# Regrouping the heads of an mLSTM kernel so that S runs in four quarter tiles, with one transfer for q and k, two state copies, and an earlier zeroing of the output

## The chip, the cores and the metric

The kernel runs on 1 core of one Trainium2 chip. The metric is the device time of one execution in microseconds (us). Before the change the median of 3 runs is 236.06 us (235.61 to 236.2).

## What is computed

The reference is a recurrent attention over 4 batches, 8 heads, 768 steps and a head width of 40, followed by a mixture of 8 experts:

```python
for t in range(S):
    m_new = np.maximum(f_gate[:, :, t] + m, i_gate[:, :, t])
    f_stab = np.exp(f_gate[:, :, t] + m - m_new)
    i_stab = np.exp(i_gate[:, :, t] - m_new)
    C = f_stab * C + i_stab * outer(v, k)          # per head, 40 x 40
    n = f_stab * n + i_stab * k
    y[:, :, t] = sigmoid(o_gate) * (C @ q) / max(abs(n @ q), 1)
...
logits = x @ w_gate                                # x: 3072 tokens of 320
expert_idx = np.argmax(logits, axis=1)
for e in range(8):
    # of the tokens of expert e the 80 with the largest gate weight are kept
    h = np.maximum(x[tok_idx] @ w1[e], 0.0)
    out[tok_idx] = gate_w * (h @ w2[e])            # all other rows stay 0
```

## The kernel before

**The work.** The recurrence is done in 12 chunks of 64 steps. The 32 heads stand as 16 groups g of two members y; the members of a group lie in the two 64-row halves of the 128 partitions. A half-step i is one chunk and 8 of the groups (16 heads), so there are 24 half-steps. For each of them there are these steps, named as in the order strings:

- `s` (`s_s`, L384): S = k·q of the 64 x 64 steps of each head, 16 matmuls. Their weights are 128 rows, in which the rows of the other member are zeros, so that the 128 rows of the moving side may hold both members' q. They run in tiles of 128 rows and 64 columns; y picks the column half. The result stands in one of two rotating banks.
- `w` (`s_arg`, L364): the decay weights, a matmul `ar` of two small tables `lh` and `rc`, and an exp on ACT. The tables come by way of DRAM: DVE makes `lb`, `store_d2` (L324) writes it out, `load_lh` (L329 to L332) and `load_rc` (L346) read it back in other shapes.
- `p` (`s_p`, L398): P = S times w, on DVE. `pv` (`s_pv`, L406): P times v, 8 matmuls of 82 columns. `int` (`s_int`, L418): q times the state, 8 matmuls of 82 columns. `st` (`s_st`, L427): the state's increment.
- `post` (`s_post`, L435 to L450): the two parts added, divided and gated, on DVE and POOL. `state` (`s_state`, L477 to L487): the new state `cs`, and four copies of 40 x 164 that put it as `cb` in the form that `int` takes; ACT makes them, or DVE and POOL in the half-steps of `OFF`.
- `tp`, `xt`, `z`, `lg`: transposes, their copies, and the gate logits; `xd` (L534) stores y to DRAM for the gather later.

**The inputs.** `load_qk` (L127 to L130) loads a chunk's q and k with two DMAs of 40 partitions x 8 KB, one for each member; three buffers rotate. Since the weights of `s` are read with all their 128 rows, the rows that no DMA writes must be zero: the function `zeros` (L158 to L170) writes those gaps once for each of the three buffers, the pieces dealt out to DVE (L164), ACT (L168) and POOL (L170). `load_kv` (L134 to L136) loads k and v in natural form, into two rotating buffers.

**The order.** It is written by hand. The string `PRE` orders the first half-steps and all that is made once, the string `BODY` is run for i = 2 to 21, and `TAIL` orders the last two half-steps. In a `BODY` of half-step i, `s` makes S of i+2 and `p` makes P of i+1. Every engine takes its instructions in that order; all DMAs but a few are issued by SP, which takes its rows in order too and holds back a row, and all rows behind it, until the row's semaphores are there. After `TAIL` comes the choice of the tokens (DVE and PE), four weight loads (L155), `zero_out` (L769 to L771: four DMAs of 960 KB that fill the output with zeros), the gather of the chosen rows by 8 indirect DMAs of POOL (L972), and the two expert layers (L1002 to L1064), whose results are scattered into the zeroed output.

The functions that the change touches, and what calls them:

Of the kernel before, what the change touches and what calls it, by code (L numbers as in the profile page):

```python
# [72 lines left out]
def tile_mlstm_moe(ctx, tc, cap, qk_d, kn_d, vn_d, og_d, if_d, cst_d, cs2_d, zr_d, wz_d, w1_d, w2_d, out_d, dbg=None):  # L73
# [53 lines left out]
    def load_qk(c):  # L127
        j = c % NQ
        SP.dma_start(qk_b[j][0:40, 0:2], qk_d[c, 0])
        SP.dma_start(qk_b[j][64:104, 1:3], qk_d[c, 1])  # L130
# [26 lines left out]

    def zeros(eng, t, *spans):  # L158
        for r0, r1, a, b in spans:
            d = t[r0:r1, a:b].rearrange("r a g t -> r (a g t)") if len(t.shape) == 4 else t[r0:r1].rearrange("r g t -> r (g t)")  # L160
            if eng is V:
                z = zb.bitcast(F32)[r0:r1]
                d = d.rearrange("r (k n) -> r k n", n=z.shape[1])
                V.tensor_copy(d, z.unsqueeze(1).broadcast_to(list(d.shape)))  # L164
            elif eng is A:
                z = zb[r0:r1]
                d = d.rearrange("r (k n) -> r k n", n=z.shape[1])
                A.copy(d, z.unsqueeze(1).broadcast_to(list(d.shape)))  # L168
            else:
                eng.memset(d, 0.0)  # L170
# [213 lines left out]
    def s_s(i):  # L384
        c, hb = divmod(i, 2)
        qk = qk_b[c % NQ]
        sp = ps.tile([128, 4, 2, T], F32, tag="s", name=f"s{i}")
        for q in range(4):
            for x in range(2):
                g = 8 * hb + 2 * q + x  # L390
                for y in range(2):
                    TE.matmul(sp[64 * y:64 * y + 64, q, x], lhsT=qk[:, 2 * y, g], rhs=qk[:, 1, g], start=True, stop=True)  # L392
# [1 line left out]
        st["p", i] = (pp, sp.rearrange("r q x t -> r (q x) t"))

    def s_p(i):
        pp, sp = st["p", i]
        V.tensor_tensor(pp, sp, st.pop(("w", i)), ALU.mult)  # L398

    def s_pv(i):  # L400
        c, hb = divmod(i, 2)
        pp, _ = st.pop(("p", i))
        hp = (ps if i == NHS - 1 else ps1).tile([128, 4, 2, V1], F32, tag="s" if i == NHS - 1 else "h", name=f"h{i}")
        for p in range(8):
            r0 = 64 * (p % 2)
            TE.matmul(hp[r0:r0 + 64, p // 2], lhsT=pp[:, p], rhs=vb[c % NV][:, :, 8 * hb + p], start=True, stop=True)  # L406
# [64 lines left out]
    def s_state(i):  # L471
        c, hb = divmod(i, 2)
        if c == NC - 1:
            return
        gs = gs_(i)
        if c:
            V.tensor_tensor(cs[:, 4 * hb:4 * hb + 4], cpv, st.pop(("cg", i)), ALU.add)  # L477
        else:
            V.tensor_copy(cs[:, 4 * hb:4 * hb + 4], cpv)
        cbv = cb.rearrange("r y (q x) v -> r y q x v", x=2)  # L480
        for x in range(2):
            for y in range(2):
                dst, src = cbv[64 * y:64 * y + 40, y, 4 * hb:4 * hb + 4, x], cs[64 * x:64 * x + 40, 4 * hb:4 * hb + 4, y]
                if i in OFF:
                    (V if x == y else P).tensor_copy(dst, src)
                else:
                    A.copy(dst, src)  # L487
# [281 lines left out]
    def zero_out(k):  # L769
        SP.dma_start(out_d.rearrange("(p r) d -> p (r d)", p=128)[:, 1920 * k:1920 * (k + 1)].rearrange("p (r n) -> p r n", n=480),  # L770
                     zt.unsqueeze(1).broadcast_to([128, 4, 480]))  # L771
# [338 lines left out]

def constants():
# [93 lines left out]
```

## Time and profile before

| | |
|---|---|
| median of 3 runs | 236.06 us |
| the profiled execution | 237.19 us |
| its span, first to last instruction | 235.4 us |
| mean granted TensorE clock | 0.901 |
| busy: PE, DVE, ACT, POOL | 197.7, 132.4, 92.3, 102.4 us |
| DMA | 52.13 MB, mean 221 GB/s |

The profile comes from one execution. PE is TensorE's matmuls, PEld its weight loads, DVE VectorE, ACT ScalarE, POOL GpSimd, and SPq the queue of DMA issues of SyncE. A row of the timeline gives the start and the duration in us, the engine, the line of the kernel, the operation, what it writes and reads, the tile or shape, and how many instructions the row gathers; in brackets stands idle time ahead of it, with what ended it. A row of SPq shows when a DMA was issued, not when it landed. By its stages the execution is: about 0 to 30 us the first half-steps and all that is made once, 30 to 78 and 78 to 131 the half-steps in `BODY`, 131 to 142 the tail, 142 to 162 the choice of the tokens, then the gather and the experts.

### The profile page before, as it was taken

The page shows a single profiled execution, that of the slowest core. Times are in us where ns is not written, and L with a number is a line of the kernel's source. Part 1 is how long each engine was busy: PE and PEld are TensorE (multiplying, and loading weights), DVE is VectorE, ACT ScalarE, POOL GpSimd, SP SyncE. Part 2 cuts the span into 40 slices and gives each one's busy share as a digit, 9 for nine tenths or more (in the row PEclk, how much of TensorE's full clock was granted, in tenths as well). Part 3 has the DMA queues.
Part 4 walks back from the last instruction along what each step waited for, and adds up shares of the span by engine and source line. Part 5 has one row for each costly group of instructions (what it writes and reads, how often), then busy time and mean ns, then how long its engine had stood idle before and what let it go on. Part 6 is the DMA issues. An engine that isn't in the chain of part 4 may idle for free. (4 is left out here: it accounts for less than half of the span.)

```text
span 235.4 us, 7898 instructions
## 1 busy us (share of the span) xinstructions
PE 197.7 (84%) x3315; PEld 147.2 (63%) x3315; DVE 132.4 (56%) x394; ACT 92.3 (39%) x215; POOL 102.4 (44%) x169
## 2 busy tenths in 40 slices
PE   6695766988695999989899887789549999999991
PEld 2375556766584788778687764434339964699540
DVE  8999855898494396998689988773000001000000
ACT  4657614679463886536455533000012210022000
POOL 8955743868576077567627514003720001110111
PEclk9659977999999799999999999555958999999998
DMA  4976389978997977869999349999379999900010
GB/s 116 230 224 135 96 187 226 256 184 226 232 248 192 225 218 176 190 165 217 320 248 284 98 95 380 421 361 383 98 227 426 424 421 414 405 35 3 0 58 14
DMA packets 21968, 52.13 MB, mean 221 GB/s; under 512 B 4972, under 2 KB 13996, under 8 KB 19180
## 3 DMA queue, kind: packets, MB, share of 16 engines
q1 hardware_dynamic: 21116, 49.72, 69.6%
q0 software_dynamic: 672, 1.64, 2.2%
q8 instruction: 26, 0.43, 0.8%
q10 hardware_dynamic: 144, 0.26, 0.4%
q14 instruction: 10, 0.08, 0.1%
HBM read 42.65 MB, written 9.12 MB: 220 GB/s over the span
## 5 line engine op out<-in xcount | busy, mean ns | idle before, releaser
L392 PEld LDWEIGHTS s<-qk 128*64 128x64 f32 x768 | 27.8, 154 | 12.5 <-issue 4.7
L392 PE MATMUL s<-qk 128*64 128x64 f32 x768 | 31.2, 242 | 4.7 <-DMA qk<-in_qk 3.7
L1064 POOL DMA_INDIRECT out<-ob,iqi x6 | 5.8, 975 | 54.3 <-DVE ob L1061 40.6
L1025 PE MATMUL hp<-cx,w 128*64 128x80 f32 x512 | 25.1, 242 | 4.2 <-DVE cx L1004 3.7
L450 POOL TENSOR_TENSOR xn<-u,rd 128x320 f32<-128x320 f32 x23 | 17.1, 747 | 25.3 <-DVE u L449 22.2
L487 ACT COPY cb<-cs 40x164 f32<-40x164 f32 x76 | 25.1, 330 | 6.7 <-DVE cs L477 4.5
L1025 PEld LDWEIGHTS hp<-cx,w 128*64 128x64 f32 x512 | 23.6, 144 | 4.7 <-DVE cx L1004 3.9
L1057 PE MATMUL op<-w,ht 128*64 128x320 f32 (+1 forms) x256 | 26.4, 433 | 0.0
L381 POOL TENSOR_TENSOR kw<-kv,w 128x320 f32<-128x320 f32 x22 | 17.1, 778 | 14.5 <-DMA kv<-in_kn 8.2
L1061 DVE TENSOR_SCALAR ob<-op,iq 128x320 f32<-128x320 f32 (+1 forms) x6 | 3.1, 523 | 33.1 <-PE op L1057 33.1
L406 PE MATMUL h<-kv,p 128*64 128x82 f32 x384 | 19.1, 242 | 1.9 <-DVE p L398 1.4
L1057 PEld LDWEIGHTS op<-w,ht 128*64 128x64 f32 (+1 forms) x256 | 12.6, 117 | 12.7 <-issue 4.3
L1044 ACT ACTIVATE ht<-hp 128x320 f32<-128x320 f32 x16 | 7.0, 437 | 33.1 <-PE hp L1025 33.1
L418 PE MATMUL hib<-cb,qk 128*64 128x82 f32 x336 | 16.5, 240 | 2.8 <-issue 2.8
L366 ACT ACTIVATE w<-ar 128x512 f32<-128x512 f32 x22 | 13.1, 596 | 13.5 <-PE ar L364 13.3
L517 ACT COPY xt<-tp 128x384 f32<-128x384 f32 x20 | 9.5, 476 | 22.1 <-PE tp L502 22.0
L406 PEld LDWEIGHTS h<-kv,p 128*64 128x64 f32 x384 | 16.6, 143 | 2.3 <-issue 2.3
L435 DVE TENSOR_TENSOR hs<-hib,gn 128x328 f32<-128x328 f32 x21 | 10.4, 496 | 13.1 <-PE hib L418 12.9
L398 DVE TENSOR_TENSOR p<-s,w 128x512 f32<-128x512 f32 x24 | 16.4, 682 | 2.0 <-ACT w L366 1.1
L427 PE MATMUL cps<-kv,kw 128*40 128x82 f32 x352 | 17.2, 239 | 0.0
L972 POOL DMA_INDIRECT xg<-xd,idx x8 | 7.9, 982 | 19.3 <-DVE gi L980 17.2
L418 PEld LDWEIGHTS hib<-cb,qk 128*64 128x64 f32 x336 | 14.0, 140 | 3.3 <-issue 3.0
(213 smaller groups left out, 370.6 us busy)
## 6 DMA issues: line engine op xcount, KB each, us to landing
w<-in_w SPq DMA_DIRECT2D x14, 1280.0 KB
qk<-in_qk SPq DMA_DIRECT2D x24, 320.0 KB
kv<-in_vn SPq DMA_DIRECT2D x24, 164.0 KB
kv<-in_kn SPq DMA_DIRECT2D x12, 320.0 KB
xd<-xn SPq DMA_DIRECT2D x24, 160.0 KB
out<-zt SPq DMA_DIRECT2D x4, 960.0 KB
xn<-in_og SPq DMA_DIRECT2D x9, 320.0 KB
w<-in_w SPq DMA_DIRECT2D x4, 640.0 KB
```

The lines of the kernel that those rows point to most:

```text
L366: A.activation(w, ar, AF.Exp)
L381: P.tensor_tensor(kw, kn_b[c % NV][:, gs_(i)], st["w", i][:, :, T - 1:T].broadcast_to([128, 8, D]), ALU.mult)
L392: TE.matmul(sp[64 * y:64 * y + 64, q, x], lhsT=qk[:, 2 * y, g], rhs=qk[:, 1, g], start=True, stop=True)
L398: V.tensor_tensor(pp, sp, st.pop(("w", i)), ALU.mult)
L406: TE.matmul(hp[r0:r0 + 64, p // 2], lhsT=pp[:, p], rhs=vb[c % NV][:, :, 8 * hb + p], start=True, stop=True)
L418: TE.matmul(hi[r0:r0 + 64, p // 2], lhsT=qk_b[c % NQ][:, 1, g], rhs=cb[:, :, g], start=True, stop=True)
L427: TE.matmul(cpv[r0:r0 + 40, p // 2], lhsT=kw[:, p], rhs=vb[c % NV][:, :, 8 * hb + p], start=True, stop=True)
L435: V.tensor_tensor(hs, st.pop(("hi", i)), gn[:, c, gs].rearrange("r (q a) -> r q a", a=2).unsqueeze(3).broadcast_to([128, 4, 2, V1]), ALU.mult)
L450: P.tensor_tensor(xn[:, i], u, rd.broadcast_to([128, 8, D]), ALU.mult)
L487: A.copy(dst, src)
L1025: TE.matmul(out, lhsT=w[:, k, c0:c0 + 64], rhs=rhs, start=start, stop=stop)
L1057: TE.matmul(o[gw * j:gw * j + m, 0:DM], lhsT=hts[p][:, f, a, t0:t0 + m], rhs=w[:, a, f], start=(f == 0), stop=(f == 7), tile_position=(0, ...
```

## The change

**q and k.** On the host q and k are padded to 64 rows for each member and stacked, so a chunk is one array of 128 rows x 8 KB. It is loaded by one DMA (1 MB instead of 2 x 320 KB; chunk 0 by two, each with half of the groups). The function `zeros`, its constants and its nine entries in `PRE` are gone.

**S.** A matmul of S now takes the 40 rows of one member alone, and is put on a quarter of the array: the row half is y, the column half is h. In a row of the program y changes first, then h, so that four neighbours lie on four quarters. The heads are regrouped for this on the host and in the constant tables. S no longer has rotating banks: one tile `spb` of two banks holds both half-steps of a chunk, and y picks the bank.

**What follows from the grouping.** `s_pv` and `s_st` write their 82 columns as two runs of 41; in `s_pv` the column half now goes 0, 0, 1, 1 over its eight matmuls instead of 0, 1, 0, 1. `s_state` needs two copies of 40 x 328 instead of four of 40 x 164. The last half-step's PV goes to `spb`.

**The zeroing.** The four DMAs of `zero_out` move from behind the four weight loads to a new step `zero` of `BODY`, behind `xd`, at i = 20.

```diff
     def load_qk(c):
-        j = c % NQ
-        SP.dma_start(qk_b[j][0:40, 0:2], qk_d[c, 0])
-        SP.dma_start(qk_b[j][64:104, 1:3], qk_d[c, 1])
+        if c:
+            SP.dma_start(qk_b[c % NQ], qk_d[c])
+            return
+        for h in range(2):
+            SP.dma_start(qk_b[0][:, :, 8 * h:8 * h + 8], qk_d[0, :, :, 8 * h:8 * h + 8])
...
     def s_s(i):
...
-        sp = ps.tile([128, 4, 2, T], F32, tag="s", name=f"s{i}")
-        for q in range(4):
+        for b in range(2):
             for x in range(2):
-                g = 8 * hb + 2 * q + x
-                for y in range(2):
-                    TE.matmul(sp[64 * y:64 * y + 64, q, x], lhsT=qk[:, 2 * y, g], rhs=qk[:, 1, g], start=True, stop=True)
+                for h in range(2):
+                    for y in range(2):
+                        r = slice(64 * y, 64 * y + D)
+                        g = 8 * hb + 4 * b + 2 * h + x
+                        TE.matmul(spb[64 * h:64 * h + 64, y, hb, 2 * b + x], lhsT=qk[r, 0, g], rhs=qk[r, 1, g], start=True, stop=True)
...
     def s_pv(i):
...
         for p in range(8):
-            r0 = 64 * (p % 2)
-            TE.matmul(hp[r0:r0 + 64, p // 2], lhsT=pp[:, p], rhs=vb[c % NV][:, :, 8 * hb + p], start=True, stop=True)
+            b, x, y = p // 4, p // 2 % 2, p % 2
+            TE.matmul(hp[64 * x:64 * x + 64, 2 * b:2 * b + 2, y], lhsT=pp[:, p], rhs=vb[c % NV][:, :, 8 * hb + p], start=True, stop=True)
...
     def s_st(i):
...
-            r0 = 64 * (p % 2)
-            TE.matmul(cpv[r0:r0 + 40, p // 2], lhsT=kw[:, p], rhs=vb[c % NV][:, :, 8 * hb + p], start=True, stop=True)
+            b, x, y = p // 4, p // 2 % 2, p % 2
+            TE.matmul(cpx[64 * y:64 * y + 40, b, :, x], lhsT=kw[:, p], rhs=vb[c % NV][:, :, 8 * hb + p], start=True, stop=True)
...
     def s_state(i):
...
-        cbv = cb.rearrange("r y (q x) v -> r y q x v", x=2)
-        for x in range(2):
-            for y in range(2):
-                dst, src = cbv[64 * y:64 * y + 40, y, 4 * hb:4 * hb + 4, x], cs[64 * x:64 * x + 40, 4 * hb:4 * hb + 4, y]
-                if i in OFF:
-                    (V if x == y else P).tensor_copy(dst, src)
-                else:
-                    A.copy(dst, src)
+        for y in range(2):
+            r = slice(64 * y, 64 * y + 40)
+            dst, src = cb[r, y, 8 * hb:8 * hb + 8], cs[r, 4 * hb:4 * hb + 4].rearrange("r q x v -> r (q x) v")
+            if i in OFF:
+                (V if y else P).tensor_copy(dst, src)
+            else:
+                A.copy(dst, src)
...
+    def b_zero(i):
+        if i == ZO:
+            for k in range(4):
+                zero_out(k)
...
-    for k in range(4):
-        zero_out(k)
```

How the instructions stand now is shown at three places. A name is that of a buffer with a number; `[waits ...]` names the engines or DMA queues whose semaphores the row waits for.

The first is SP's queue at the start of the program, before: `gt` is the gates, `d` the DRAM copy of `lb`.

```order
L92 DMA gt<-in_gif 32x1536
L129 DMA qk_81<-in_qk 40x2048 [waits DVE_49]
L130 DMA qk_81<-in_qk 40x2048 [waits Pool_49]
L134 DMA kv_84<-in_kn 128x640
L324 DMA d_133<-lb 32x6x128 [waits DMAHW1_49,DVE_49]
L129 DMA qk_83<-in_qk 40x2048 [waits DMAHW2_49,Pool_49]
L130 DMA qk_83<-in_qk 40x2048 [waits DMAHW3_49,Pool_49]
L129 DMA qk_81<-in_qk 40x2048 [waits DMAHW4_49,PE_49]
L346 DMA rc_93<-d_133 3x16x128 [waits DMAHW6_49,DMAHW1_49,DVE_49]
```

The same queue now (the rows for chunk 1 lie between the fourth and the fifth in both):

```order
L92 DMA gt<-in_gif 32x1536
L134 DMA qk_81<-in_qk 128x2x512 x2
L138 DMA kv_84<-in_kn 128x640
L312 DMA d_134<-lb 32x6x128 [waits DVE_49]
L131 DMA qk_83<-in_qk 128x2048 [waits DMAHW1_49]
L131 DMA qk_81<-in_qk 128x2048 [waits DMAHW2_49,PE_49]
L334 DMA rc_94<-d_134 3x16x128 [waits DMAHW3_49,DMAHW0_49,DVE_49]
```

The transfers of q and k wait for no zeroing by DVE, POOL or ACT any more, and the rows for `rc` and `lh` behind them don't either.

The second is DVE in a half-step of `BODY`, from one state update (`cs`) to the next, before:

```order
L477 TENSOR_TENSOR cs<-cps,cg_1150 104x328 [waits Pool_49]
L398 TENSOR_TENSOR p_1113<-s_1096,w_1084 128x512 [waits Activation_49]
L435 TENSOR_TENSOR hs_1262<-hib,gn 128x328 [waits PE_49]
L437 TENSOR_TENSOR hs_1262<-h_1234,hs_1262 128x328 [waits DVE_49,PE_49]
L443 TENSOR_SCALAR rd_1265<-hs_1262 128x8 [waits DVE_49]
L445 TENSOR_TENSOR rd_1265<-hs_1262,rd_1265 128x8 [waits DVE_49]
L447 RECIPROCAL rd_1265<-rd_1265 128x8 [waits DVE_49]
```

The same stretch now:

```order
L470 TENSOR_TENSOR cs<-cps,cg_1102 104x328 [waits Pool_49]
L388 TENSOR_TENSOR p_1066<-spb,w_1040 128x512 [waits PE_49,Activation_49]
L428 TENSOR_TENSOR hs_1211<-hib,gn 128x328 [waits PE_49]
L430 TENSOR_TENSOR hs_1211<-h_1183,hs_1211 128x328 [waits DVE_49,PE_49]
L436 TENSOR_SCALAR rd_1214<-hs_1211 128x8 [waits DVE_49]
L438 TENSOR_TENSOR rd_1214<-hs_1211,rd_1214 128x8 [waits DVE_49]
L440 RECIPROCAL rd_1214<-rd_1214 128x8 [waits DVE_49]
```

No row moved, but `p` of half-step i+1 now waits for PE as well: the last matmul of S of i+2, which PE has written to the same two banks just ahead.

The third is SP's queue at the end of `BODY`, before (`zt` is the tile of zeros, `w` the experts' weights):

```order
L155 DMA w_0_1713<-in_w 128x1280
L134 DMA kv_85<-in_kn 128x640
L136 DMA kv_85<-in_vn 64x656 x2
L534 DMA xd<-xn 64x4x160 x6
L155 DMA w_1_2496<-in_w 128x2560 x2
L155 DMA w_0_2499<-in_w 128x2560 x2
L770 DMA out<-zt 128x4x480 x4
L981 DMA gid<-gi 96x16
```

The same stretch now:

```order
L159 DMA w_0_1644<-in_w 128x1280
L138 DMA kv_85<-in_kn 128x640
L140 DMA kv_85<-in_vn 64x656 x2
L526 DMA xd<-xn 64x4x160 x2
L756 DMA out<-zt 128x4x480 x4
L526 DMA xd<-xn 64x4x160 x4
L159 DMA w_1_2409<-in_w 128x2560 x2
L159 DMA w_0_2412<-in_w 128x2560 x2
L969 DMA gid<-gi 96x16
```

The zeros stand ahead of the last four stores of y and of four of the weight loads.

More of the change, by code (lines that the diff above doesn't have):

```diff
@@ L40 @@
 WH = [2, 0, 1, 0]
-BODY = "tab pr0 cmp s int pv tp st load xt xd cg p w post arg0 pr1 cnt pg z state d2 arg1 sig lh og lg"
+BODY = "tab pr0 cmp s int pv tp st load xt xd zero cg p w post arg0 pr1 cnt pg z state d2 arg1 sig lh og lg"
 PG = {11: (8, 10), 3: (4, 6), 9: (6, 8), 12: (10, 12)}
@@ L59 @@
 BW0 = [2, 2, 2, 2, 4]
+ZO = 20
 GATE = {7: (0, 2), 13: (2, 4), 15: (4, 6), 19: (6, 8), 21: (8, 9)}
@@ L100, in tile_mlstm_moe @@
     NV, NQ = 2, 3
-    qk_b = [cp.tile([128, 3, G16, T], F32, name=f"qk{i}") for i in range(NQ)]
+    qk_b = [cp.tile([128, 2, G16, T], F32, name=f"qk{i}") for i in range(NQ)]
     kv_b = [cp.tile([128, 2, VN + KN], F32, name=f"kv{i}") for i in range(NV)]
@@ L107, in tile_mlstm_moe @@
     cs = cp.tile([104, 8, 2, V1], F32, name="cs")
+    spb = ps1.tile([128, 2, 2, 4, T], F32, tag="s", name="spb")
     cps = ps1.tile([128, 512], F32, tag="cps", name="cps")
@@ L156, in load_w @@
             yield
[L158 to L168, printed above, removed]
-            else:
-                eng.memset(d, 0.0)
-    GAPS = ((32, 64, 0, 2), (64, 128, 0, 1), (96, 128, 1, 3), (0, 64, 2, 3))
     zb = gp.tile([128, 512], BF16, name="zb")
@@ L386, in s_s @@
         qk = qk_b[c % NQ]
[L387 to L388 removed]
+        for b in range(2):
             for x in range(2):
[L390 to L392 removed]
+                for h in range(2):
[3 more added lines that the diff above has]
+                        TE.matmul(spb[64 * h:64 * h + 64, y, hb, 2 * b + x], lhsT=qk[r, 0, g], rhs=qk[r, 1, g], start=True, stop=True)
         pp = wk.tile([128, 8, T], F32, tag="p", name=f"p{i}")
[L394 removed]
+        st["p", i] = (pp, spb[:, :, hb].rearrange("r y f t -> r f y t"))
     def s_p(i):
         pp, sp = st["p", i]
[L398 removed]
+        two = lambda a: a.rearrange("r (f y) t -> r f y t", y=2)
+        V.tensor_tensor(two(pp), sp, two(st.pop(("w", i))), ALU.mult)
     def s_pv(i):
@@ L402, in s_pv @@
         pp, _ = st.pop(("p", i))
-        hp = (ps if i == NHS - 1 else ps1).tile([128, 4, 2, V1], F32, tag="s" if i == NHS - 1 else "h", name=f"h{i}")
+        if i == NHS - 1:
+            hp = spb.rearrange("r y h f t -> r (y h f t)")[:, 0:8 * V1].rearrange("r (q y v) -> r q y v", y=2, v=V1)
+        else:
+            hp = ps1.tile([128, 4, 2, V1], F32, tag="h", name=f"h{i}")
         for p in range(8):
-            r0 = 64 * (p % 2)
-            TE.matmul(hp[r0:r0 + 64, p // 2], lhsT=pp[:, p], rhs=vb[c % NV][:, :, 8 * hb + p], start=True, stop=True)
+            b, x, y = p // 4, p // 2 % 2, p % 2
+            TE.matmul(hp[64 * x:64 * x + 64, 2 * b:2 * b + 2, y], lhsT=pp[:, p], rhs=vb[c % NV][:, :, 8 * hb + p], start=True, stop=True)
         st["h", i] = hp
@@ L798, in tile_mlstm_moe @@
                 z=b_z, state=s_state, pr1=b_prep(1), cmp=b_cmp, cnt=b_cnt, lg=b_lg, arg1=b_arg1, sig=s_sig, xd=b_xd, pg=b_pg,
-                load=b_load, lh=b_lh, og=b_og, d2=b_d2, tab=b_tab, w=b_w)
+                load=b_load, lh=b_lh, og=b_og, zero=b_zero, d2=b_d2, tab=b_tab, w=b_w)
     for i in range(2, NHS - 2):
@@ L1108, in constants2, with heads @@
     return c
+def heads(a):
+    return a.transpose(0, 2, 3, 1, *range(4, a.ndim)).reshape(32, *a.shape[4:])
 def constants():
@@ L1143, in constants @@
     put("dy", 0, dy.reshape(32, 2))
-    put("sel", 0, sel.reshape(32, 48))
-    put("ind", 0, ind.reshape(32, 104))
+    put("sel", 0, heads(sel.reshape(B, 2, 2, 2, 48)))
+    put("ind", 0, heads(ind.reshape(B, 2, 2, 2, 104)))
     return c
```

23 lines of the change are left out of this document (9 added, 14 removed).

## The prediction

> **What bounds the kernel now.** I read the busy time by stages first, since the shares over the whole span mix stages with different limits. The columns are PE, PEld, DVE, ACT and POOL busy, then PE's granted clock, the share of the DMA engines' time and GB/s.
>
> ```profile
> core 0: us, PE busy (x) PEld busy (x) DVE busy (x) ACT busy (x) POOL busy (x), PEclk, DMA share, GB/s
> 10.00:20.00 10.00, 8.81 (x102) 6.26 (x101) 9.75 (x22) 6.95 (x8) 7.21 (x7) 0.60 0.88 228
> 20.00:30.00 10.00, 6.72 (x147) 5.67 (x147) 8.71 (x31) 6.21 (x17) 6.11 (x9) 1.00 0.40 101
> 30.00:40.00 10.00, 6.41 (x95) 5.59 (x97) 5.26 (x11) 2.35 (x6) 2.63 (x5) 0.75 0.85 183
> 60.00:70.00 10.00, 8.20 (x182) 6.75 (x184) 7.04 (x25) 5.16 (x14) 6.21 (x18) 1.00 0.97 249
> 80.00:90.00 10.00, 10.00 (x223) 8.37 (x220) 8.03 (x22) 8.49 (x14) 5.94 (x12) 1.00 0.87 217
> 100.00:110.00 10.00, 9.10 (x208) 7.63 (x210) 9.06 (x34) 4.48 (x11) 6.39 (x13) 1.00 0.76 186
> 130.00:140.00 10.00, 8.64 (x155) 6.88 (x152) 9.14 (x38) 4.33 (x13) 3.24 (x5) 1.00 0.25 65
> 150.00:160.00 10.00, 7.88 (x61) 3.86 (x60) 7.16 (x18) 0.00 (x0) 0.00 (x0) 0.50 1.01 381
> ```
>
> Three limits follow one another. From 10 to 20 us DVE has no gap (9.75 of 10). From 30 to about 78 no engine is full and the DMA engines nearly are. From 80 on PE has no gap (10.00 of 10), with DVE at 8 to 9 behind it. In the timeline of the first stage the reader is to see the zero writes between the steps of the gate scan, and whom they hold up:
>
> ```profile
> 1.16 3.89 DVE L164 COPY qk<-zb 32x2048 f32<-32x2048 f32 x2
> 5.78 0.28 DVE L290 TENSOR_TENSOR_SCAN m<-gt 32x64 f32<-32x64 f32 x1
> 13.96 0.69 DVE L164 COPY qk<-zb 64x1024 f32<-64x1024 f32 x1
> 16.74 1.88 DVE L164 COPY qk<-zb 64x1024 f32<-64x1024 f32 x1
> 22.93 0.27 DVE L318 TENSOR_TENSOR lb<-rb,lb 32x128 bf16<-32x128 f32 x1
> 4.58 1.35 ACT L660 COPY xg<-cst 32x1024 f32<-32x1024 f32 x2 [1.92 <-DMA cst<-in_cst]
> 25.52 1.80 POOL L170 MEMSET qk<- 32x2048 f32 x1
> 23.23 0.33 SPq L324 DMA_DIRECT2D d<-lb  x1
> 23.66 0.32 SPq L129 DMA_DIRECT2D qk<-in_qk  x1
> 27.34 0.29 SPq L130 DMA_DIRECT2D qk<-in_qk  x1
> 28.49 1.46 SPq L346 DMA_DIRECT2D rc<-d  x2
> 31.69 1.97 PE L392 MATMUL s<-qk 128*64 128x64 f32 x32 [3.67 <-DMA qk<-in_qk]
> 37.71 0.10 PEld L364 LDWEIGHTS <-lh 118*128 118x128 bf16 x1 [2.06 <-DMA lh<-d]
> 75.07 0.10 PEld L364 LDWEIGHTS <-lh 118*128 118x128 bf16 x1 [2.90 <-DMA lh<-d]
> ```
>
> The store of `lb` is issued at 23.23, when DVE has made the last of it (22.93 + 0.27). The second q/k transfer of chunk 2 sits at SP until POOL's zeros end at 25.52 + 1.80 = 27.32, and the reads of `rc` and `lh` stand behind it. PE then waits for q/k until 31.69 and for `lh` until 37.71, and again until 75.07.
>
> One half-step of the stage that PE bounds, from the timeline, with the first and the last of the twelve starts of S in it:
>
> ```profile
> 78.03 1.78 PE L392 MATMUL s<-qk 128*64 128x64 f32 x32
> 91.82 1.15 PE L392 MATMUL s<-qk 128*64 128x64 f32 x32
> 91.98 1.40 ACT L487 COPY cb<-cs 40x164 f32<-40x164 f32 x4
> 92.14 0.68 DVE L398 TENSOR_TENSOR p<-s,w 128x512 f32<-128x512 f32 x1
> 92.80 0.74 PE L418 MATMUL hib<-cb,qk 128*64 128x82 f32 x16
> 93.37 0.74 PE L406 MATMUL h<-kv,p 128*64 128x82 f32 x16
> 93.59 0.50 DVE L435 TENSOR_TENSOR hs<-hib,gn 128x328 f32<-128x328 f32 x1 [0.77 <-PE hib L418]
> 94.04 0.55 PE L502 MATMUL tp<-cst,xn 128*128 128x128 f32 x3
> 95.22 0.63 PE L525 MATMUL tp<-xt,wz 128*32 128x128 f32 x12
> 95.78 0.39 PE L364 MATMUL ar<-rc,lh 118*128 118x512 bf16 x1
> 127.89 1.15 PE L392 MATMUL s<-qk 128*64 128x64 f32 x32
> ```
>
> Since the ends of matmuls are modelled, I take a block's length from its start to the next start: S 0.98 us (32 records, two for each matmul), `int` 0.57 and PV 0.67 (16 records each).
>
> **The change part by part.** The sum is made against the profiled execution, 237.19 us, of which 235.4 is its span. The median of the runs is 1.13 lower, and I take that off at the end.
>
> *Zeros on DVE.* The 3.89 us ahead of the scan go. The gates must still land. ACT got `cst` at 4.58; it is 253 KB by the page's list of DMA issues,
>
> ```profile
> cst<-in_cst ACTq DMA_DIRECT2D x1, 253.0 KB
> ```
>
> and the gates, issued by SP at the same start, are 32 x 1536 words or 192 KB. So by their bytes the gates are there at about 4.58 x 0.76 = 3.5 (an estimate), and 5.78 becomes about 3.5: 2.3 gained (bounds 1.2, were they as late as `cst`, and 3.89). The other two copies, 0.69 + 1.88 = 2.57, lie in the full stretch, so the store at 23.23 comes 4.9 earlier. The pieces on ACT and the early ones on POOL I cost at nothing: in row 10 to 20 neither is full (6.95 and 7.21).
>
> *SP's wait for POOL.* From 23.66 + 0.32 = 23.98 to 27.34 SP stood still: 3.36 more. The reads of `rc` and `lh` are thus issued 8.2 us earlier, and S at 31.69 can keep up, its wait of 3.67 being of that transfer.
>
> *The bytes.* A chunk's q and k grow from 640 KB to 1 MB, by 0.39 million bytes. The transfers ahead of the read of `lh` that PE gets at 75.07 are those of chunks 2 to 6, five. At the 381 GB/s of the full queue (row 150 to 160) each costs 1.03 us more, at the 249 GB/s of row 60 to 70 (DMA share 0.97) 1.58. I take 1.03: the growth is in long rows, and the 249 is a mix with many short ones. So 8.2 - 5 x 1.03 = 3.1 us are left when the stage ends (bounds 8.2, if the idle DMA time of row 20 to 30, share 0.40, takes them all, and 8.2 - 5 x 1.58 = 0.3).
>
> *S on PE.* Two column halves take 16 rounds of 0.98 / 16 = 0.061 us. No row of before uses row halves, so the cost is bounded: eight rounds, 0.49, if four quarters work side by side; sixteen, 0.98, if row halves take turns but column halves still pair; thirty-two, 1.95, if the order (y first) lets no two overlap. That PE can keep four tiles busy is shown by L525: 12 records of 128 columns on four tiles of 32 columns start 0.56 before the next block, 0.047 each, while S takes 0.031 for half of the columns. I take eight rounds: -0.49.
>
> *Change of tile shape.* Now S and `int` share the 128x64 shape. PV, ahead of a change to `tp`, takes 0.67 against 0.57 for the same 16 records of `int`: a change costs 0.10, and S now has one more.
>
> *PV.* Its rounds of 0.57 / 8 = 0.071 us pair neighbouring column halves. In the order 0, 0, 1, 1 the 16 records take between 8 rounds, if PE reaches past a neighbour, and 13, if records pair only where the half changes (three times). I take 10, +0.14, nearer to 8 because L525's tiles alternate as freely.
>
> *Two runs of 41 columns.* No matmul of before writes its result in two runs. The bounds are nothing and the cost of two matmuls: from 64 columns at 0.061 and 82 at 0.071, 41 come to 0.048, so a round takes 0.096 and the 16 rounds of PV and `st` 0.40 more. I take nothing, as each run is long.
>
> [...]
>
> *Sum on PE.* -0.49 + 0.10 + 0.14 = -0.25 for a half-step. The twelve make 3.0 us; of these I count two thirds, 2.0, because DVE at 8 to 9 of 10 sometimes ends last.
>
> *DVE's new wait.* `p` at 92.14 must now wait for S, at the latest to 92.80. Behind it on DVE is `hs`, which stood idle 0.77 for `int` until 93.59; `p` would end at 92.80 + 0.68 = 93.48, so the idle time covers it. Without that cover it costs 0.66 in every half-step.
>
> *State copies.* 1.40 on ACT becomes two of about 0.5 (like the 0.50 for `hs`, 328 columns). ACT bounds no stage: nothing.
>
> *The zeroing.* These rows show the end:
>
> ```profile
> 141.65 15.57 SPq L770 DMA_DIRECT2D out<-zt  x4
> 162.12 1.16 POOL L972 DMA_INDIRECT xg<-xd,idx  x1 [17.19 <-DVE gi L980]
> 167.99 0.24 PEld L1002 LDWEIGHTS xp<-cst,xg 80*128 80x128 f32 x3 [2.21 <-DMA xg<-xd,idx]
> 171.15 0.96 POOL L972 DMA_INDIRECT xg<-xd,idx  x1 [0.31 <-issue]
> 173.75 0.32 DVE L1004 COPY cx<-xp 128x160 f32<-128x160 f32 x1 [4.98 <-remote]
> ```
>
> The zeros are issued until 141.65 + 15.57 = 157.2, behind four weight loads of 1280 KB. These 5.24 million bytes and the zeros' 3.93 take 24.1 us at 381 GB/s, from about 140 to 164, so zeros still flow when the gather starts at 162.12; its first rows reach PE at 167.99. The last S before the tail, at 127.89, is that of i = 21. Moved to i = 20, some 4 us ahead of it, and with about 4 us gained by then, they flow from about 120 for 3.93 / 0.381 = 10.3 us and longer where others share the queue, a good part of it in row 130 to 140, where the DMA share is 0.25. What is queued behind them on SP is four stores of y and four weight loads, which the gather needs only 20 us later. The last gather is issued at 171.15 and DVE stands until 173.75, so I think the gather's own pace decides, not its start: 0.7 gained, of at most 167.99 - 162.12 - 3 = 2.9 if a gather without traffic takes 3 us (an estimate from 171.15 to 173.75).
>
> Together 3.1 + 2.0 + 0.7 = 5.8: 237.19 - 5.8 = 231.4, and 1.13 less is a median of **230.3**.
>
> **The rivals.**
>
> 1. *The bytes are free.* For it: the idle DMA time before 30. Against it: share 0.97 later. Then 8.2 + 2.0 + 0.7 = 10.9 go: 225.2 (222.0 if S gives its full 3.0 and the gather 2.9).
> 2. *The bytes cost 1.58 each.* For it: the 249 GB/s. Then 0.3 + 2.0 + 0.7 = 3.0: 233.1.
> 3. *Row halves take turns, columns pair.* S stays 0.98, and a half-step grows by 0.10 + 0.14 = 0.24, or 2.9 in twelve: 3.1 + 0.7 - 2.9 = 0.9 go, so 235.2, at the border of what can be measured.
> 4. *Nothing overlaps in S: slower.* For it: y changes first, so neighbours always differ in the row half, and PE starts records in order. S takes 1.95, a half-step grows by 0.97 + 0.24 = 1.21, 14.5 in all, against 3.8 gained elsewhere: +10.7, 246.8. It decides from 3.8 / 12 = 0.32 a half-step, that is, from an S of 0.98 + 0.32 - 0.24 = 1.06 us. Against it: L525.
> 5. *Two runs cost two matmuls.* +0.40 x 12 = 4.8 against 5.8: 235.1.
>
> That the change doesn't do what it says is case 3.
>
> **How the numbers follow.** Chances: forecast 0.48, with its own range 228 to 232.5; the rivals 0.15, 0.10, 0.12, 0.08 and 0.07. A measurement of this kernel tells 0.3% apart, so the borders are 235.35 and 236.77. Faster: 0.48 + 0.15 + 0.10, and half of cases 3 and 5, 0.09: 0.82. Within: a quarter of those two, 0.05. Slower: case 4 and the last quarter, 0.13. The range goes down into case 1 as far as 223.5 and up through cases 3 and 5 to 236.8; outside lie case 4 and the ends of 1 and 3.
>
> **What would show it.** Right: the scan starts at about 3.5, S of chunk 2 waits for no q/k, and `lh` ends PE's wait about 6 us before 37.7 (8.2 less two loads of 1.03) and 3 before 75; S takes 0.5 to 0.6 us from its start to `int`, PV 0.7 to 0.8; no zeros flow after 150. Wrong: S at 0.98 or over 1.06 (cases 3 and 4), PV and `st` both longer by 0.2 (case 5), waits for `lh`, `rc` or k and v longer than before from 40 to 80 (case 2), or DVE without idle time ahead of `hs`.

## The result, and the profile after

The changed kernel takes 226.45 us (median of 4 runs, 224.75 to 228.12), against 236.13 for the kernel before on the same chip: a ratio of 0.9587, with a 95% interval of 0.9523 to 0.965. It is 9.7 us faster, where 5.8 was forecast. Some executions of one kernel on one chip are 1 to 2% slower than the rest; the ratios leave them out, the medians and ranges do not. The profiled execution took 228.12 us with a span of 226.3, the slowest of the four. In two other profiles of the same program, from other chips, the first gather is issued at 153.62 and 153.09 us, against 153.76 here, so up to there this one is like them, and the comparison below goes by places in the program.

| place | before | after | gained |
|---|---|---|---|
| first step of the gate scan | 5.78 | 4.14 | 1.64 |
| first S | 10.39 | 10.42 | 0.0 |
| store of `lb` for chunks 2 and 3 | 23.23 | 20.70 | 2.5 |
| issue of the reads of `rc` | 28.49 | 22.37 | 6.1 |
| S of half-step 4 | 31.69 | 27.21 | 4.5 |
| PE's load of `lh`, first long wait | 37.71 | 31.93 | 5.8 |
| PE's load of `lh`, third | 75.07 | 67.45 | 7.6 |
| S of half-step 12 | 78.03 | 70.67 | 7.4 |
| S of half-step 23, the last | 127.89 | 118.89 | 9.0 |
| issue of the first gather | 162.12 | 153.76 | 8.4 |
| end of the span | 235.4 | 226.3 | 9.1 |

In the busy time by stages of the changed kernel (columns as before: five engines, PE's clock, DMA share, GB/s) the reader is to see that the DMA engines move more bytes a second than before: 270 GB/s at a share of 0.81 in row 20 to 30, where 101 at 0.40 stood before, 323 at 0.99 in row 50 to 60 (213 at 0.85), and 254 at 0.77 in row 80 to 90 (217 at 0.87).

```profile
20.00:30.00 10.00, 6.83 (x125) 5.44 (x127) 6.82 (x21) 4.20 (x13) 4.71 (x7) 0.85 0.81 270
50.00:60.00 10.00, 9.32 (x216) 7.35 (x214) 9.71 (x28) 6.33 (x16) 7.02 (x17) 1.00 0.99 323
80.00:90.00 10.00, 10.00 (x246) 7.80 (x240) 7.98 (x28) 5.33 (x15) 6.36 (x13) 1.00 0.77 254
```

The first stage in its timeline: the zero writes are gone, and the gates arrive at 4.14. The second step of the scan now runs beside POOL's making of `rc` and takes 1.92 instead of 0.28 us. Later DVE stands 2.50 us for PV.

```profile
4.14 0.28 DVE L278 TENSOR_TENSOR_SCAN m<-gt 32x64 f32<-32x64 f32 x1 [2.35 <-DMA gt<-in_gif]
5.08 1.92 DVE L285 TENSOR_TENSOR_SCAN lc<-mask,lf 32x64 f32<-32x64 f32 x1
4.96 1.89 POOL L238 TENSOR_TENSOR rc<-cst 118x1024 bf16<-118x1024 f32 x1
9.61 0.18 DVE L287 CAST lb<-lc 32x64 bf16<-32x64 f32 x1
11.12 0.47 DVE L278 TENSOR_TENSOR_SCAN m<-gt,m 32x128 f32<-32x128 f32 x1
16.24 0.50 DVE L432 COPY hs<-h 128x328 f32<-128x328 f32 x1 [2.50 <-PE h L399]
20.70 0.35 SPq L312 DMA_DIRECT2D d<-lb  x1
21.09 0.91 SPq L131 DMA_DIRECT2D qk<-in_qk  x2
22.37 1.49 SPq L334 DMA_DIRECT2D rc<-d  x2
27.21 1.13 PE L381 MATMUL spb<-qk 40*64 40x64 f32 x32 [2.86 <-DMA qk<-in_qk]
67.45 0.10 PEld L352 LDWEIGHTS <-lh 118*128 118x128 bf16 x1 [2.83 <-DMA lh<-d]
```

Before, the same operation of POOL stood beside another step of DVE, a cast that took 1.74 us where it takes 0.18 now. So this loss only moved, and the next scan, that of 32 x 128, starts 13.46 - 11.12 = 2.3 us earlier; these are the rows of before:

```profile
9.58 1.74 DVE L299 CAST lb<-lc 32x64 bf16<-32x64 f32 x1
13.46 0.47 DVE L290 TENSOR_TENSOR_SCAN m<-gt,m 32x128 f32<-32x128 f32 x1
9.38 1.89 POOL L250 TENSOR_TENSOR rc<-cst 118x1024 bf16<-118x1024 f32 x1
```

The half-step that PE bounds, from the same timeline: S is 0.62 us from its start to `int` (0.98 before), `int` 0.62 (0.57), PV 0.72 (0.67).

```profile
80.50 0.69 PE L381 MATMUL spb<-qk 40*64 40x64 f32 x32
81.12 0.79 PE L411 MATMUL hib<-cb,qk 128*64 128x82 f32 x16
81.74 0.79 PE L399 MATMUL h<-kv,p 128*64 128x82 f32 x16
82.46 0.55 PE L494 MATMUL tp<-cst,xn 128*128 128x128 f32 x3
```

### The profile page after: what moved, and what is told of

The parts are those of the page before. It is cut to its first block, busy times and chain, and to the rows that moved or that the text cites. A ratio compares the mean times of both kernels' runs of the same rounds, so it can differ in the third digit from the quotient of the medians.

```text
span 226.3 us, 7831 instructions
## 1 busy us (share of the span) xinstructions
PE 193.6 (86%) x3312; PEld 140.7 (62%) x3315; DVE 127.5 (56%) x387; ACT 80.6 (36%) x174; POOL 93.0 (41%) x161
## 3 DMA queue, kind: packets, MB, share of 16 engines
q0 software_dynamic: 672, 1.64, 2.3%
## 5 line engine op out<-in xcount | busy, mean ns | idle before, releaser
L1013 PEld LDWEIGHTS hp<-cx,w 128*64 128x64 f32 x512 | 24.6, 147 | 3.7 <-issue 3.0
L381 PEld LDWEIGHTS spb<-qk 40*64 40x64 f32 x768 | 15.3, 151 | 10.8 <-DMA qk<-in_qk 3.0
L381 PE MATMUL spb<-qk 40*64 40x64 f32 x768 | 18.9, 244 | 2.9 <-DMA qk<-in_qk 2.9
L479 ACT COPY cb<-cs 40x328 f32<-40x328 f32 x38 | 17.6, 463 | 10.3 <-DVE cs L470 8.5
L388 DVE TENSOR_TENSOR p<-spb,w 128x512 f32<-128x512 f32 x24 | 16.4, 685 | 8.0 <-PE spb L381 7.2
L411 PE MATMUL hib<-cb,qk 128*64 128x82 f32 x336 | 18.2, 250 | 2.5 <-issue 1.7
L420 PE MATMUL cps<-kv,kw 128*40 128x82 f32 x352 | 18.0, 246 | 0.0
L420 PEld LDWEIGHTS cps<-kv,kw 128*40 128x40 f32 x352 | 14.0, 122 | 5.2 <-DVE rd L438 1.6
L1013 PE MATMUL hp<-blk,w 128*64 128x160 f32 (+1 forms) x136 | 16.6, 315 | 0.7 <-issue 0.7
L354 ACT ACTIVATE w<-ar 128x512 f32<-128x512 f32 x22 | 13.1, 595 | 11.0 <-PE ar L352 10.8
L494 PE MATMUL tp<-cst,xn 128*128 128x128 f32 x72 | 14.3, 313 | 3.1 <-POOL xn L443 1.3
```

The source lines that it names most:

```text
L354: A.activation(w, ar, AF.Exp)
L381: TE.matmul(spb[64 * h:64 * h + 64, y, hb, 2 * b + x], lhsT=qk[r, 0, g], rhs=qk[r, 1, g], start=True, stop=True)
L388: V.tensor_tensor(two(pp), sp, two(st.pop(("w", i))), ALU.mult)
L411: TE.matmul(hi[r0:r0 + 64, p // 2], lhsT=qk_b[c % NQ][:, 1, g], rhs=cb[:, :, g], start=True, stop=True)
L420: TE.matmul(cpx[64 * y:64 * y + 40, b, :, x], lhsT=kw[:, p], rhs=vb[c % NV][:, :, 8 * hb + p], start=True, stop=True)
L494: TE.transpose(tp[:, k], xf[:, XB[k]:XB[k] + 128], ident)
```

## The experiments

The chips differ: the kernel before has a median of 236.13, 232.5, 231.72 and 236.92 us on the four used here. Times are therefore compared within one chip, and places in the program across chips, since up to the gather they agree within 2 us (in three profiles of the changed kernel S of half-step 12 starts at 70.67, 70.87 and 68.79, S of half-step 20 at 105.26, 105.21 and 103.46). A smaller difference of such places is not read as an effect. Theory: the gain comes from the zero writes and from moving q and k in transfers that cover all 128 partitions; S in four quarters adds a smaller part. The rival is the prediction's own account, in which the added bytes cost 1.03 us a chunk.

**The changed kernel again,** as a measure for the next three.

> The changed kernel itself, as the measure for the three beside it: 224.7 to 228.2 us, as in its four runs. Both theories expect the same.

Measured: 220.18 us (219.29 to 220.94), ratio 0.9454 (0.9396 to 0.9513) to before.

**The zero writes put back.**

```diff
-PRE = "msk lq0 ad0 ..."
+PRE = "qb msk qa lq0 ad0 ..."
...
+        qa=lambda: zeros(V, qk_b[0], *GAPS[0:2]), qb=lambda: zeros(P, qk_b[0], *GAPS[2:4]),
...
+        qd0=lambda: zeros(V, qk_b[2], GAPS[1]), qd1=lambda: zeros(P, qk_b[2], GAPS[0]),
```

> The changed kernel with the zero writes of before put back into the q/k buffers (the same pieces on DVE, POOL and ACT; the loads overwrite them, so they only cost time). The prediction put them at 4.9 on DVE and 3.36 on SP, 8.2 together, of which the changed profile shows 6.1 at the reads of rc and lh and 5.8 at the first wait for lh: about 226.5 + 6 = 232.5. The rival, that the stage from 30 to 78 takes most of it back because DMA bounds it: not over 2 us, 228.5.

Measured: 225.52 us (224.97 to 226.07), 5.3 slower than the changed kernel on this chip. The timeline of SP and PE shows the same two delays as in the kernel before: the store of `lb` at 25.18, and the transfer of q and k held back 4 us behind it.

```profile
25.18 0.34 SPq L329 DMA_DIRECT2D d<-lb  x1
29.49 0.82 SPq L132 DMA_DIRECT2D qk<-in_qk  x2
30.42 1.45 SPq L351 DMA_DIRECT2D rc<-d  x2
34.44 1.13 PE L398 MATMUL spb<-qk 40*64 40x64 f32 x32 [3.38 <-DMA qk<-in_qk]
```

The changed kernel beside it, on the same chip:

```profile
20.36 0.35 SPq L312 DMA_DIRECT2D d<-lb  x1
20.76 0.91 SPq L131 DMA_DIRECT2D qk<-in_qk  x2
22.04 1.45 SPq L334 DMA_DIRECT2D rc<-d  x2
```

The reads of `rc` are 8.4 later with the zeros, S of half-step 4 is 7.3 later (34.44 against 27.12), that of half-step 12 5.6, the gather 4.0. So the zeros are worth about what the prediction put on them, and the stage behind gives back a third; the rival's 2 us at most is out.

**Fewer bytes, in the old shape.**

```diff
     def load_qk(c):
+        if c > 2:
+            for y in range(2):
+                r = slice(64 * y, 64 * y + D)
+                SP.dma_start(qk_b[c % NQ][r], qk_d[c, r])
+            return
```

> The changed kernel with q and k of chunks 3 to 11 loaded as before, by two transfers of 40 rows (the padding stays zero from the first three loads): 0.39 million bytes less for each of nine chunks. The prediction's step, that a byte more costs 1.03 us a chunk in the full queue: four such chunks lie ahead of the last read of lh, so about 4 us faster, 222.5. The rival, read from the changed profile (a lone 1 MB transfer moves about 0.4 million bytes a us, a lone 40-row one of before about 0.2): the rows decide and not the bytes, so the time stays or grows by up to 4, 226.5 to 230.5.

Measured: 226.75 us (225.63 to 228.77), 6.6 slower than the changed kernel. The prediction's account of the bytes is out: nine loads with 0.39 million bytes less each make the kernel slower. The load of `lh` waits twice as long (third wait; in the changed kernel 2.32 on this chip):

```profile
50.41 0.10 PEld L357 LDWEIGHTS <-lh 118*128 118x128 bf16 x1 [4.01 <-DMA lh<-d]
72.94 0.10 PEld L357 LDWEIGHTS <-lh 118*128 118x128 bf16 x1 [4.80 <-DMA lh<-d]
```

**The same bytes, in two transfers of 64 rows.**

```diff
         if c:
-            SP.dma_start(qk_b[c % NQ], qk_d[c])
+            for y in range(2):
+                r = slice(64 * y, 64 * y + 64)
+                SP.dma_start(qk_b[c % NQ][r], qk_d[c, r])
             return
```

> The changed kernel with each q/k load as two transfers of 64 rows, the same bytes. If the number of rows in flight decides how fast a transfer moves, two of 64 queued one behind the other move nearly like one of 128: 226.5, within 0.5. If a transfer of 64 rows uses only part of the queue's width, as one of 40 does, the loads take longer: 1 to 3 us more, 228 to 229.5. If it is the number of SP rows and semaphores that costs, likewise about 1 more.

Measured: 242.33 us (239.18 to 244.61), ratio 1.0538 (1.0453 to 1.0623): slower than the kernel before, on a chip where that takes 231.72. No theory had as much, though the second had the kind. What a transfer moves a second is read from stretches in which little else than q and k is under way, by the busy time in windows (last columns: DMA share, GB/s). Before, chunks 2 and 3 in transfers of 40 rows:

```profile
24.00:26.00 2.00, 2.00 (x40) 1.53 (x40) 1.23 (x3) 1.64 (x2) 1.22 (x2) 1.00 0.60 172
28.50:30.50 2.00, 0.00 (x0) 0.00 (x0) 1.79 (x4) 0.12 (x2) 2.00 (x5) 1.00 0.56 164
```

The changed kernel, the same chunks in transfers of 128 rows:

```profile
23.00:27.00 4.00, 1.35 (x33) 1.19 (x32) 2.40 (x7) 1.85 (x7) 3.40 (x6) 0.99 1.01 391
```

The experiment, in transfers of 64 rows:

```profile
27.50:32.50 5.00, 5.00 (x72) 4.35 (x70) 2.69 (x8) 1.19 (x5) 2.91 (x5) 0.50 0.98 210
```

391 GB/s against 210 and 168 (the mean of 172 and 164): a transfer over all partitions moved about twice as fast here, with the same length of row. At these rates (an estimate) a chunk took 655,360 bytes / 168 GB/s = 3.9 us before, takes 1,048,576 / 391 = 2.7 now, and 5.0 in halves. The added bytes are not paid for; by this estimate the wide transfer saves 1.2 us a chunk in the queue.

Both experiments also load a chunk by two transfers instead of one. That this is not what costs shows in chunk 0, which the changed kernel loads by two transfers as well, but each over all partitions. In the window from 4 to 6 us, in which its packets of 2 KB move almost alone, its second profile has 339 GB/s:

```profile
4.00:6.00 2.00, 1.63 (x4) 0.30 (x2) 1.81 (x4) 1.40 (x3) 1.32 (x2) 1.00 0.98 339
```

What in the shape sets the pace is not shown. That a transfer of 64 rows keeps to a part of the queue, as the second theory has it, does not show in the share: it is 0.98 there at 210 GB/s, 0.60 and 0.56 with 40 rows at 172 and 164, and 1.01 with 128 rows at 391.

**S without row halves side by side.**

```diff
-        for b in range(2):
-            for x in range(2):
-                for h in range(2):
-                    for y in range(2):
+        for y in range(2):
+            for b in range(2):
+                for x in range(2):
+                    for h in range(2):
```

> The changed kernel with the loop over y outermost in S, so that neighbours differ in the column half alone and row halves never run side by side within a pair. If four quarters side by side are what shortens S, S goes from 0.62 us to its next block back to about 1.08 (16 rounds of 0.058 and a change of shape), 0.45 more in each of 12 to 14 half-steps that PE bounds: 226.5 + 5.5 = 232, or + 3.7 if a third is hidden behind DVE. The rival, that the hardware finds row-half neighbours farther ahead, or that PE does not bound: not over 1 us, 227.5.

Measured: 222.4 us (221.1 to 224.85), ratio 0.9626 (0.9536 to 0.9716). The changed kernel did not run on this chip, and of its three ratios on the others (0.9454 to 0.9606) two have intervals that meet this one's, so the time decides nothing. The timeline does:

```profile
81.28 0.98 PE L381 MATMUL spb<-qk 40*64 40x64 f32 x32
82.19 0.79 PE L411 MATMUL hib<-cb,qk 128*64 128x82 f32 x16
```

S takes 0.91 to `int` instead of 0.62, with the same matmuls and shapes: neighbours on four quarters run side by side, and the order makes them so. It is less than the 1.08 expected: 13 rounds of 0.058 instead of 16, and 0.15, make 0.90. That three of its rounds still hold records of both values of y, where the loop turns, is an estimate from these times. From S of half-step 13 to that of 20 the profile has 30.5 us, against 29.4, 29.4 and 29.8 in three profiles of the changed kernel: 0.7 to 1.1 in seven half-steps, so the time gets about half of the 0.29, or less.

**PV's order.**

```diff
-        for p in range(8):
+        for p in (0, 2, 1, 3, 4, 6, 5, 7):
             b, x, y = p // 4, p // 2 % 2, p % 2
             TE.matmul(hp[64 * x:64 * x + 64, 2 * b:2 * b + 2, y], ...
```

> The changed kernel with PV's eight matmuls in an order in which the column half alternates again. In the changed profile PV takes 0.72 to the next block against 0.67 before, one round more. Theory: the order costs that round, 0.05 a half-step, 0.7 in all: 225.8. Rival: the two runs of 41 columns cost it, then PV stays at 0.72 and the time at 226.5.

Measured: 222.36 us (220.4 to 225.05), ratio 0.9606 (0.9509 to 0.9703), undecided, as the changed kernel did not run on this chip. The timeline shows PV back at 0.67 (83.42 to 84.09), so the order costs the round and the two runs of 41 columns cost nothing: before, with one run of 82, it was 0.67 as well. The prediction's fifth case, in which PV and `st` would each be 0.2 longer, is out: `st` takes 0.70 as well (84.56 to 85.26), as before (94.52 to 95.22). PV here:

```profile
83.42 0.73 PE L399 MATMUL h<-kv,p 128*64 128x82 f32 x16
84.09 0.55 PE L494 MATMUL tp<-cst,xn 128*128 128x128 f32 x3
```

**The zeroing back at the end, and the zeroing alone.**

```diff
-ZO = 20
+ZO = 99
...
+    for k in range(4):
+        zero_out(k)
```

> The changed kernel with the zeroing of the output back behind the four weight loads. The prediction's step: 0.7 us slower, 227.2. First rival: 1.8 slower, 228.3, since in the changed profile the first copy of gathered rows comes 1.8 us sooner after the gather's issue. Second rival: up to 1.4 faster, 225, since the changed profile loses 1.4 us of its gain from half-step 21 to the gather, while the zeros flow.

Measured: 220.49 us (219.67 to 220.68), 0.3 more than the changed kernel, within both spreads. Its first copy of gathered rows takes longer to come after the gather's issue: 157.80 - 151.87 = 5.9 against 158.04 - 153.62 = 4.4, so the early zeroing wins about 1.5 there, as the first rival has it. Its gather is also issued 1.75 earlier, but the second rival is not shown by that: S of half-step 22 starts at 114.37 against 116.14, 1.77 earlier, and the changed kernel issues its first zeros only at 118.34. From S of half-step 22 to the gather both take 37.5. So in the whole the early zeroing is worth something between nothing and 1.5, and the four runs of each do not tell which. The two timelines, POOL's and DVE's rows, first without the early zeroing:

```profile
151.87 1.16 POOL L963 DMA_INDIRECT xg<-xd,idx  x1 [17.20 <-DVE gi L971]
157.80 0.32 DVE L995 COPY cx<-xp 128x160 f32<-128x160 f32 x1 [5.94 <-PE xp L993]
```

And the changed kernel:

```profile
153.62 1.16 POOL L960 DMA_INDIRECT xg<-xd,idx  x1 [17.19 <-DVE gi L968]
162.67 0.96 POOL L960 DMA_INDIRECT xg<-xd,idx  x1 [0.31 <-issue]
158.04 0.33 DVE L992 COPY cx<-xp 128x160 f32<-128x160 f32 x1 [4.42 <-PE xp L990]
159.45 0.33 DVE L992 COPY cx<-xp 128x160 f32<-128x160 f32 x1 [1.09 <-PE xp L990]
```

```diff
-BODY = "... load xt xd cg ..."
+BODY = "... load xt xd zero cg ..."
...
+    def b_zero(i):
+        if i == 20:
+            for k in range(4):
+                zero_out(k)
...
-    for k in range(4):
-        zero_out(k)
```

> The kernel before with the zeroing alone moved to i = 20. The prediction's step: 0.7 us faster than before, 235.4. First rival: 1.8 faster, 234.3 (the gather's first rows come sooner). Second rival: no gain or slower, up to 237.5, because the zeros crowd the loads and stores of the last half-steps.

Measured: 230.4 us (227.1 to 231.35), ratio 0.9903 (0.9848 to 0.9958), 2.2 faster than before by that ratio and 1.3 between the medians, a gain of about 1%. Its first copy comes 167.77 - 162.93 = 4.8 after the gather's issue, against 168.45 - 162.12 = 6.3 in the profile of the kernel before, the same 1.5 as in the changed kernel. Why the time shows it in this kernel and not in the changed one stays open. A full queue is not the reason: from 120 to 130 us the DMA share of the changed kernel is 1.03 with the zeros and 0.23 with the zeros at the end.

**The state copies.**

```diff
-            dst, src = cb[r, y, 8 * hb:8 * hb + 8], ...
+            for k in range(2):
+                dst, src = cb[r, y, 8 * hb + 4 * k:8 * hb + 4 * k + 4], ...
...
-                (V if y else P).tensor_copy(dst, src)
+                    (V if y == k else P).tensor_copy(dst, src)
...
```

The measure for this one and the next two:

> The changed kernel itself, as the measure for the three beside it: 219 to 228 us, by the chip. Both theories expect the same.

Measured: 226.81 us (225.71 to 228.73), ratio 0.9606 (0.955 to 0.9663).

> The changed kernel with the state copied in four pieces of 40 x 164 again. The prediction's step: ACT bounds no stage, so nothing, within 0.7 us of the changed kernel. Rival: the copies end last before int, most of all in the half-steps of OFF on DVE, 0.3 to 0.4 each where PE waits for them: 1 to 3 us slower.

Measured: 227.06 us (224.94 to 228.75), 0.25 from the changed kernel, far within both spreads: nothing.

**The first weight loads later.**

```diff
-        if 15 <= i < 23:
+        if 19 <= i < 23:
             next(lw[0], 0)
...
+    run(lw[0])
     wp = st["wp"]
```

> The changed kernel with the first four weight loads (640 KB each) moved from i = 15 to 18 to i = 19 and later, behind the last load of k and v. Theory: since PE got faster, the DMA queue, full from 100 to 112, is what half-steps 19 to 21 wait for (S of 22 starts 7.0 after S of 21 in the second profile of the changed kernel, 4 to 5 elsewhere): 2 to 3 us faster. Rival: the waits are for something else, or come back because the last stores of y stand behind zeros and weights: within 0.7, or slower.

Measured: 224.59 us (223.77 to 226.3), ratio 0.9505 (0.945 to 0.9559), 2.2 under the changed kernel on that chip; the two intervals just meet, and five of its six runs are below the fastest of the changed kernel's six. In the changed kernel's second profile S of half-step 22 starts 7.0 after that of 21 (4.7 in its first, 7.2 in its third, on this chip), while weights are in the queue, as the timeline of SP and PE shows:

```profile
107.74 0.60 SPq L159 DMA_DIRECT2D w<-in_w  x1
109.10 0.69 PE L381 MATMUL spb<-qk 40*64 40x64 f32 x32
111.39 0.65 PE L411 MATMUL hib<-cb,qk 128*64 128x82 f32 x12 [1.30 <-issue]
116.14 0.69 PE L381 MATMUL spb<-qk 40*64 40x64 f32 x32
```

Its busy time in the window from 100 to 112 ends with a DMA share of 1.03:

```profile
100.00:112.00 12.00, 10.70 (x260) 8.46 (x260) 9.86 (x27) 6.28 (x13) 7.81 (x14) 1.00 1.03 332
```

With the weights later it is 4.1 in the timeline, the share in the same window 0.73, and the gather is issued at 151.28 instead of 153.09 to 153.76, 1.8 us earlier than in the third profile:

```profile
109.12 0.69 PE L381 MATMUL spb<-qk 40*64 40x64 f32 x32
113.23 0.69 PE L381 MATMUL spb<-qk 40*64 40x64 f32 x32
```

```profile
100.00:112.00 12.00, 12.00 (x286) 9.62 (x286) 11.21 (x33) 6.52 (x14) 8.55 (x15) 1.00 0.73 234
```

It has the lowest median on its chip, 12.3 us under the kernel before. The gain is there, but the theory's reason for it is not shown. The profile of the next run, which has the weights late too, has the long half-step again, 7.2 from S of 21 to S of 22, at a DMA share of 0.80 from 100 to 112 (that execution took 228.34 us, the median of its kernel is 225.24):

```profile
109.65 0.69 PE L381 MATMUL spb<-qk 40*64 40x64 f32 x32
112.09 0.85 PE L411 MATMUL hib<-cb,qk 128*64 128x82 f32 x12 [1.46 <-issue]
116.84 0.69 PE L381 MATMUL spb<-qk 40*64 40x64 f32 x32
```

Both long half-steps are made of the same two parts. PE stops in the middle of `int`, for 1.30 and 1.46 us, and no semaphore ends the stop; then its granted clock is 0.50, from 112 to 115 in the one and from 113 to 115 in the other. The trace also has the packets of a DMA queue called "instruction", 16 KB each. One of them ends at 110.05 in the first case and at 110.73 in the second, and PE goes on 1.34 and 1.36 later; with the late weights alone it ends at 108.70, and PE does not stop. In the fourteen profiles of this case all 28 such stops of PE's matmuls (0.4 us or more, between 20 and 140 us) end 1.3 to 1.7 us after a packet of that queue; in the kernel before, for one, the stops end at 61.80 and 101.98 and the packets at 60.34 and 100.32. So PE probably waits for its own instructions there, an inference from these times; whether it was the weights that held them up is not shown.

> The same with PV's column half alternating as well. PV's order alone brought S of half-step 20 from 105.2 to 102.7 and lost it again by S of 22. Theory: without the queue's wait this is kept, 2 to 3 us faster than with the late weights alone. Rival: the gain before was chance, 0.05 a half-step is all, 0.7 faster.

Measured: 225.24 us (224.34 to 228.34), ratio 0.9532 (0.9486 to 0.9579): no different from the late weights alone, so the second theory's 2 to 3 us are out. PV's round is too small to be measured in the whole.

## Why the prediction was right, and where it was not

The direction and two of the three sources were right, the third (the zeroing) is not shown in the time. The size was too small by 3.9 us in the median: 226.45 lies outside the forecast's own 228 to 232.5, nearer to the 225.2 of the first rival, and only the wider range from 223.5 takes it in. One step is to blame for more than the 3.9.

- **Zeros on DVE and SP's wait: right in kind.** Forecast were 8.2 us at the reads of `rc` and `lh`; against the kernel before they came 6.1 earlier, and 8.4 earlier than with the zeros put back. The start came about as forecast: the gates came at 4.14, not 3.5, but by the scan of 32 x 128 the gain is 2.3. What the sum missed is that DVE then stands 2.50 for PV, a wait that the zeros had covered: 2.3 + 2.57 - 2.50 = 2.4 of the 4.9 are left, and the store of `lb` came 2.5 earlier. SP's part is as forecast, 6.1 - 2.5 = 3.6 against 3.36.
- **The bytes: the step that failed.** "So 8.2 - 5 x 1.03 = 3.1 us are left when the stage ends" took a byte to cost the same in any transfer. Instead the gain grew from 5.8 to 7.4 in that stage, 4.3 more than forecast. A load of 128 rows moves at 391 GB/s where the two of 40 rows moved at about 168, and with the old shape put back the kernel is 6.6 slower with fewer bytes. The case of free bytes was among the rivals, with 0.15; that the wider transfer is quicker was in none. That the time came out near the case of free bytes is in part luck: less than forecast was gained at the reads, and more than nothing by the transfers. The row that could have told it was there: the window from 24 to 26 of before, where the 40-row transfers reached 172 GB/s at a share of 0.60, against the 381 GB/s of row 150 to 160.
- **PE: right, with its parts off.** -0.25 for a half-step was forecast, -0.36 + 0.05 + 0.05 = -0.26 came; that the sums agree is in part luck, as the errors of the parts cancel. S has its eight rounds, of 0.058; the change of shape costs 0.15, since the first round behind it is 0.05 slower too; PV lost one round, 0.05, where two were forecast, 0.14. From S of half-step 12 to the last, 1.6 us were gained, forecast 2.0; in the two other profiles it is 1.0 and nothing, since S of 22 comes late there. Up to S of 21 the three have 2.4, 2.7 and 1.9. That PE has no gap from 80 on was read too broadly: the prediction's own row 100 to 110 has it at 9.10 of 10.
- **DVE's new wait: right.** DVE now stands 8.0 us ahead of `p` (2.0 before) and 2.2 ahead of the first `hs` (13.1 before), together 10.2 instead of 15.1, so one wait took the place of the other. Of the 8.0, 6.2 stand at two places, 28.48 and 71.94, ahead of which S itself comes late; in the half-steps that PE bounds the new wait is 0.2 to 0.5, in three of them. The groups of instructions, before and then after, with the idle time behind the second bar:

```profile
L398 DVE TENSOR_TENSOR p<-s,w 128x512 f32<-128x512 f32 x24 | 16.4, 682 | 2.0 <-ACT w L366 1.1 <-PE s L392 0.8
L435 DVE TENSOR_TENSOR hs<-hib,gn 128x328 f32<-128x328 f32 x21 | 10.4, 496 | 13.1 <-PE hib L418 12.9
```

```profile
L388 DVE TENSOR_TENSOR p<-spb,w 128x512 f32<-128x512 f32 x24 | 16.4, 685 | 8.0 <-PE spb L381 7.2 <-ACT cb L479 0.6
L428 DVE TENSOR_TENSOR hs<-hib,gn 128x328 f32<-128x328 f32 x21 | 10.4, 493 | 2.2 <-PE hib L411 2.2
```

- **State copies: right,** as the run with four shows (227.06 us against 226.81).
- **The zeroing: the size not shown, the reason wrong.** 0.7 was forecast; the 0.3 measured lies within the spreads, so that the two are near tells nothing. What came sooner is the first copy, by 1.5. The gather's pace does not set the second copy: on one chip it came at 159.45, 3.2 before the last gather's issue at 162.67, on two others 3.8 and 4.4 us after the first copy, at 160.53 and 162.66, with "remote" as its releaser. What DVE waits for there stays open.
- **The slower rival** (nothing overlaps in S) is refuted: S is 0.62, far from 1.06.

## What to carry to other kernels

Judge a transfer by the partitions that it covers before counting its bytes: one of 128 partitions with three eighths of padding beat two of 40 here by far (391 GB/s against about 168, and by the estimate above 2.7 us a chunk against 3.9), and two of 64 were worse than either (210 GB/s, 5.0 us a chunk). Zeros that are written once cost more than their engine's time: of the 6.1 us at the reads of `rc`, 2.5 came through DVE and 3.6 through the queue rows that had waited for POOL, so count the rows behind. Loads that nothing needs soon can cost: with the weight loads of half-steps 15 to 18 moved out of a stretch with a DMA share of 1.03, this kernel was 2.2 us faster, though what they had held up is not shown.

## What the runs showed that was not expected

- Transfers of 64 rows: 210 GB/s at a DMA share of 0.98, so the share alone doesn't show how much a queue moves: with 128 rows it was 391 GB/s at 1.01. A packet of 8 KB takes 0.61 us there and 0.34 in the transfers of 128 rows.
- A DVE scan of 32 x 64 elements took 1.92 us beside a POOL operation of 1.89, and 0.28 without it. In the kernel before a cast of the same size took 1.74 beside that operation, and 0.18 in the changed one without it.
- The part behind the gather differs in the same program, in one profile from each of three chips: from the first gather's issue to the end 65.5 us on one chip, 71.7 and 72.6 on two others. On those two DVE's second copy comes late, and PE's granted clock in the 9 us from 163 on is 0.62 and 0.73 instead of 1.00. No run tried the cause.
